# A spectral filter and a gated feed-forward network in one kernel: batch 1's first transform goes through DRAM, a quarter of it inside the feed-forward loop

## The chip, the cores and the metric

The kernel runs on one core of a Trainium2 chip. The metric is the device time of one execution in microseconds. TensorE (PE, with its weight loads PEld), VectorE (DVE), ScalarE (ACT) and GpSimd (POOL) each work through their own list of instructions in order; SyncE (SP) and POOL mostly issue DMAs here. They wait for each other through semaphores.

## The reference

```
X = rfft(x, axis=1)                    # x: 8 batches, 3008 positions, 256 columns d, float32
y = irfft(X * (filt_r + 1j*filt_i))    # a filter for each frequency and d
gate = maximum(y @ w_gate, 0)          # y as 24064 tokens x 256; w_gate, w_val: 256 x 1536
out  = (gate * (y @ w_val)) @ w_out    # w_out: 1536 x 256; out: 24064 x 256, float32
```

## The kernel before

**The transform.** The 3008 positions are taken as 94 (n1) by 32 (n2). For each batch: stage A is a 94-point transform over n1, for each n2; then its result must be turned, so that n2 lies on the partitions; `fwd` is the 32-point transform (six calls, i = 0 to 5, two PSUM banks each); `product` multiplies by the filter, `add` combines real and imaginary parts; `inv` (three calls, q = 0 to 2) goes back; its result is turned again, and `item_c` does the last 94-point step, which leaves the tokens as `yT` in blocks of 512, two halves of d each.

**The feed-forward network.** There are 47 blocks of 512 tokens with 12 steps each. A step is one `gv` (four matmuls of 512 columns into psV and psG, line 555; ACT copies psV as `vsb`, line 558; DVE makes `prod`, line 560) and, from the second block on, four matmuls of `o_part` for the block before (psO, line 576). Block k+1's `item_c` stands in steps 8 and 10 of block k (4 and 6 of block 0). Other work is hung on step numbers by `at_step(s, f)`; within a step the order is gv, o_part, the hung work, item_c. The schedule is written by hand: each engine takes its instructions in the order in which this program issues them.

**Three ways through stage A.** Batch 0 does it in the prologue with one float32 matmul for 512 columns (`a_bank`, line 265), ACT copies the result out (`a_0`, line 277) and DVE turns it (`turn_0`, line 300). Batches 2 to 7 do it inside the feed-forward loop in four chunks each. A chunk holds the columns n2 = 8q+2j and 8q+2j+1; `load_chunk` fetches it as two halves, the second in reversed row order (lines 340 and 344), into XP[j], a quarter of the buffers XF; POOL folds the halves in six instructions (`fold_chunk`, lines 353 to 358); `tiled_a` runs 32 small matmuls (psF, line 367), ACT and DVE copy two banks each, and SP stores the result to a buffer in DRAM (`Abuf`, line 378). When all four are there, `load_at_tiled` reads it back turned (line 385).

Batch 1 is between the two. Its x is loaded whole in the prologue, and 16 items `a_1`, of four n2 and half of d each, are spread by `item(n)` over batch 0's transform: two before inv(0,0), two before inv(0,1), two before inv(0,2), seven behind it, three behind the two `item_c` of block 0. The lower half of d goes through DRAM (`store_half`, line 324; `load_half`, line 330), the upper half is turned by DVE in four pieces (`turn_1`, line 295), one in the prologue and three in steps 1, 7 and 12. `fwd(1, 0)` and `fwd(1, 1)` stand in step 14.

**Batch 0 around the change.** `first_b` holds its six fwd and three inv. Products go to DVE from PSUM (line 422), those of `ON_POOL` to POOL (line 420), from a copy `xs` that ACT makes (line 419). `place_own` is two small copies on POOL (line 224); the third inverse block needs them. The results of inv(0, q) are copied to `DS0` (line 458), and `turn_d` turns all of it in two halves of d (line 300). POOL then issues the weight loads (`load_vg` twice, line 245, `load_o`, line 251), which convert to bf16 on the way, copies M1 (line 664) and changes the sign of every second row of Fti (line 672). `warm(n)` is n matmuls of 512 columns on a constant tile. `hold` is a small DMA on SP that waits for a part of the filter and so holds back batch 1's x.

Of the kernel before, what the change touches and what calls it, by code (L numbers as in the profile page):

```python
# [29 lines left out]
N1, N2 = 94, 32  # L30
# [86 lines left out]
def kernel(  # L117
# [44 lines left out]
    Abuf = [dram.tile([NROW * N2, D if b > 1 else D // 2], BF16, name=f"Abuf{b}") if b else None for b in range(B)]  # L162
# [9 lines left out]
    AS1 = [dCb[:, 32:48, :].rearrange("p n d -> p (n d)").rearrange("p (l c d) -> p l c d", l=NC2, d=D // 2)]  # L172
# [21 lines left out]
    WHOLE = ((0, 0, NX2 * D), (1, 0, NX2 * D))  # L194
# [3 lines left out]
    conj32 = pro.tile([128, 2], FP32, tag="conj32", bufs=1)  # L198
# [60 lines left out]

    def a_bank(n2, nn, d0, nd):  # L260

        psA = bank("psA", nn, nd)
        xf = XF[n2 // NX2].rearrange("p (n d) -> p n d", d=D)
        n = n2 % NX2
        nc.tensor.matmul(psA, WA, xf[:, n:n + nn, d0:d0 + nd], start=True, stop=True)  # L265
        return psA

    def a_0(n2, nn, d0, nd):

        psA = a_bank(n2, nn, d0, nd)  # L270
        dq = D // 4
        l, q = n2 % NC2, slice(d0 // dq, (d0 + nd) // dq)
        c = n2 // NC2
        dst = AS0.rearrange("p q (l c) e (g f) -> p l c g q e f", c=2, g=2)[:, l:l + nn, c // 2, c % 2]
        src = psA.rearrange("p n (q e f) -> p n q e f", e=dq // 2, f=2)
        for i in range(nd // dq):
            nc.scalar.copy(dst[:, :, q.start + i], src[:, :, i])
        done(psA)

    def a_1(p, s, h):  # L280

        psA = a_bank(NC2 * p + 4 * s, 4, h * D // 2, D // 2)
        if h and len(AS1) == 1:
            for _ in range(2):
                t = sb.tile([128, NC2 * D], BF16, tag="asb", bufs=3, name="asb")
                AS1.append(t.rearrange("p (l c d) -> p l c d", l=NC2, c=N2 // NC2))
        ts = AS1[1:] if h else AS1[:1]
        w = D // 2 // len(ts)
        for i, t in enumerate(ts):
            nc.scalar.copy(t[:, 4 * s:4 * s + 4, p, :], psA[:, :, i * w:(i + 1) * w])  # L290
        done(psA)

    def turn_a(dst, src):

        nc.vector.transpose(dst.bitcast(FP32).rearrange("p k d -> p d k"),
                            src.bitcast(FP32).rearrange("p n d -> p d n"))
# [6 lines left out]
    def turn_0(q):  # L303
        w = D // 8
        turn_pairs(ats[0][:, :, q * w:q * w + w], AS0[:, q])

    def turn_1(i):
        w = D // 8
        src = AS1[1 + i // 2].rearrange("p l c d -> p (l c) d")
        turn_a(ats[1][:, 1, :, i * w:i * w + w], src[:, :, i % 2 * w:i % 2 * w + w])  # L310

    def new_at(b):
        shape = [2, 32, D // 2] if b else [16, D // 2, 4]
        ats[b] = sb.tile([128, *shape], BF16, tag="at", bufs=1, name="at")
# [6 lines left out]
    def store_half(b):  # L321
        w = N2 * D // 2
        for q in range(4):
            nc.sync.dma_start(_ap(Abuf[b], q * NG * w, [[w, NG], [1, w]]),
                              AS1[0][32 * q:32 * q + NG].rearrange("p l c d -> p (l c d)"))

    def load_half(b):
        w = N2 * D // 2
        for q in range(4):
            nc.sync.dma_start(ats[b][32 * q:32 * q + 32, 0, 0:NG, :],  # L330
                              _ap(Abuf[b], q * NG * w, [[D // 2, 32], [w, NG], [1, D // 2]]))
# [3 lines left out]
    def load_chunk(b, j, eng):  # L335

        xp = XP[j]
        for q in range(4):
            r, o = 32 * q, 8 * q + 2 * j
            eng.dma_start(xp[r:r + 24, 0:4:2, :],  # L340
                              _ap(x, (b * N1 * N2 + o) * D,
                                  [[N2 * D, 24], [47 * N2 * D, 2], [1, 512]]))
        for i in range(2):
            eng.dma_start(xp[:, 2 * i + 1, :],
                              _ap(x, ((b * N1 + 46 + 47 * i) * N2 + 2 * j) * D,
                                  [[8 * D, 4], [-N2 * D, 32], [1, 512]]))

    def fold_chunk(b, j):

        xp = XP[j]  # L350
        t = fs.tile([128, 2, 512], FP32, tag="fold", bufs=1, name="fold")
# [29 lines left out]
    def load_at_tiled(b):  # L381

        ats[b] = sb.tile([128, NG, D], BF16, tag="at", bufs=1, name="at")
        for rr in range(4):
            nc.sync.dma_start(ats[b][32 * rr:32 * rr + 32].rearrange("p j d -> p (j d)"),
                              _ap(Abuf[b], rr * N2 * NG * D, [[NG * D, 32], [1, NG * D]]))

    ON_POOL = ((0, 1), (1, 1), (2, 1))
    ats = {}
# [3 lines left out]
    def fwd(b, i):  # L393
# [4 lines left out]
        for r in range(2):  # L398
            for c in range(4):
                for e in range(2):  # L400
# [3 lines left out]
                                     ats[b][64 * e:64 * e + 64, j, :] if b > 1 else  # L404
                                     ats[b][64 * e:64 * e + 64, :, j, :] if b else
# [3 lines left out]
    def product(b, i, e, k, pool=False):  # L409
# [6 lines left out]
        if pool:  # L416
            if not k:
# [17 lines left out]
    def inv(b, q):  # L435
# [14 lines left out]
        dst = sb.tile([128, 8, D], BF16, tag="dsb", bufs=3, name="dsb") if b else DS0  # L450
        def out(cs):
            for c in cs:
                copy = nc.vector.tensor_copy if (c % 2 if b else (q, c) in ((1, 3), (2, 0), (2, 1))) else nc.scalar.copy
                if b:
                    copy(dst[:, c:8:4, :], psD[c])
                else:
                    k, g = 4 * q + c // 2, c % 2 * 2
                    copy(dst[:, k:k + 3:2, :, g:g + 2], psD[c].rearrange("p m (f e) -> p m e f", f=2))
                done(psD[c])
        if not b:  # L460
            return out(range(4))
# [10 lines left out]
    def first_b(item):  # L472

        def products(i, es=(1, 0)):
            for e in es:
                for k in range(2):
                    product(0, i, e, k, pool=(i, e) in ON_POOL)
# [19 lines left out]
        place_own()  # L497
        inv(0, 1)
        item(2)
        inv(0, 2)  # L500

# [30 lines left out]
    def item_c(k, h):  # L532
# [10 lines left out]
        if h == 0 or k:  # L543
            nc.scalar.copy(dst, psY)  # L544
        else:
            nc.vector.tensor_copy(dst, psY)
# [88 lines left out]
    new_at(0)  # L635
# [11 lines left out]
    nc.sync.dma_start(hold, Ftr[0:2, 4, 0:8])  # L647
    load_x(1, sp, ((0, 0, 2 * q), (0, 2 * q, 4 * q), (1, 0, 2 * q), (1, 2 * q, 4 * q)))
    items = iter([(p, s, h) for p in range(4) for h in range(2) for s in range(2)])

    def item(n):
        for _ in range(n):
            p, s, h = next(items)
            a_1(p, s, h)
            if (p, s, h) == (3, 1, 0):
                new_at(1)
                store_half(1)
                load_half(1)

    first_b(item)  # L660
    load_vg(0, DFF // 2)
    load_vg(DFF // 2, DFF)
    load_o()
    nc.gpsimd.tensor_copy(M1, tabs[:, 578:].rearrange("p (l n) -> p l n", l=2))
    for h in range(2):
        turn_d(h)
    item(7)
    for hh in range(2):
        item_c(0, hh)
    item(3)  # L670
    turn_1(0)
    nc.gpsimd.tensor_scalar(Fti, Fti, conj[:, 0:1], 1.0, op0=ALU.mult, op1=ALU.mult)
    nc.sync.dma_start(WF, nc.inline_tensor(fold_h, name="dft_fold").ap())
# [9 lines left out]
    for k in range(1, 4):  # L683
        at_step((1, 7, 12)[k - 1], lambda k=k: turn_1(k))
# [77 lines left out]
```

## Time and profile before

| what | value |
|---|---|
| time, median of 3 runs | 867.87 us (867.31 to 867.9) |
| the profiled execution, its own time | 865.68 us |
| its span in the profile | 863.8 us |
| TensorE busy | 848.7 us, 98% of the span |
| DVE, ACT, POOL busy | 577.8, 494.6, 458.4 us |
| first psV matmul of the feed-forward network | 45.6 us |
| first psX matmul of batch 1 | 60.44 us |

The profile is of one execution. Times in it count from the start of the span. In the rows of the timeline and of the groups stand the start, the length in us, the engine, the line of the kernel, the operation, what it writes and reads, and in brackets the idle time of the engine before it and what ended it. SPq and POOLq are the parts of those engines that issue DMAs; a matmul in float32 shows as two records.

### The profile page before, as it was taken

To read this page: it belongs to the slowest core of one execution; us is meant where nothing else is said; L and a number is where in the kernel's file an instruction comes from. 1 tells how busy PE (TensorE), PEld (TensorE's weight loads), DVE (VectorE), ACT (ScalarE), POOL (GpSimd) and SP (SyncE) were. 2 spreads that over 40 slices of the span, in tenths; PEclk is the share of its full clock that TensorE was granted. 3 is DMA by queue.
4 is the path that set the end of the run, shared out by engine and by line. 5 is a ranking of instruction groups with operands and counts; after the bars stand their busy time and mean duration, and the time that the engine had idled before them with its cause. 6 is when DMAs were issued, how large, how long until landed. Compare 5 with 4: busy or idle time off the path is not lost.

```text
span 863.8 us, 20396 instructions
## 1 busy us (share of the span) xinstructions
PE 848.7 (98%) x7587; PEld 498.8 (58%) x7704; DVE 577.8 (67%) x863; ACT 494.6 (57%) x904; POOL 458.4 (53%) x496
## 2 busy tenths in 40 slices
PE   9999999999999999999999999999999999999997
PEld 4456655656556555556556655565655656666665
DVE  3878865777657775577765787658865688555553
ACT  5765565555655556555555555555556555555552
POOL 6747890488986765776666756767450023000001
PEclk9999999999999999999999999999999999999999
DMA  9985365334782339633386333762464422611111
GB/s 250 241 164 122 96 158 138 109 113 110 190 183 88 84 87 192 166 98 98 85 208 142 95 103 100 190 151 74 101 130 108 99 58 52 126 43 29 37 35 52
DMA packets 101366, 101.61 MB, mean 118 GB/s; under 512 B 21827, under 2 KB 89955, under 8 KB 99730
## 3 DMA queue, kind: packets, MB, share of 16 engines
q1 hardware_dynamic: 81986, 77.96, 36.1%
q0 software_dynamic: 18928, 21.82, 11.7%
q8 instruction: 61, 1.00, 0.5%
q10 hardware_dynamic: 352, 0.52, 0.2%
q14 instruction: 39, 0.32, 0.1%
HBM read 58.23 MB, written 45.88 MB: 121 GB/s over the span
## 4 chain that ended last, share of the span: by engine, by line
PE 94%; DMA 2%; issue 1%; DVE 1%; ACT 1%; SPq 1%; POOL 0%; DVEq 0%; ACTq 0%
PE psG L555 29%; PE psO L576 28%; PE psV L555 26%; PE psA L265 3%; PE psF L367 3%; PE psY L538 3%; PE psD L445 2%; PE psX L402 1%; DMA XF<-in_x_dram 1%; DMA Abuf<-asb 1%; ACT vsb L558 1%; DVE prod L560 1%; SPq L190 0%; DVE tt L422 0%; DMA out_dram<-osb 0%
## 5 line engine op out<-in xcount | busy, mean ns | idle before, releaser
L560 DVE SCALAR_TENSOR_TENSOR prod<-psG,vsb 128x512 bf16<-128x512 f32 x564 | 389.4, 691 | 235.8 <-ACT vsb L558 231.6
L558 ACT CAST vsb<-psV 128x512 bf16<-128x512 f32 x564 | 332.2, 589 | 225.8 <-PE psV L555 121.1
L576 PE MATMUL psO<-WoT,prod 128*128 128x256 bf16 x2256 | 336.6, 273 | 0.8
L555 PE MATMUL psG<-yT,WgT 128*128 128x512 bf16 x1111 | 331.8, 379 | 5.2
L555 PE MATMUL psV<-yT,WvT 128*128 128x512 bf16 x1030 | 314.9, 380 | 0.1
L576 PEld LDWEIGHTS <-prod 128*128 128x128 bf16 x2256 | 220.6, 98 | 143.4
L555 PEld LDWEIGHTS <-WgT 128*128 128x128 bf16 x1128 | 110.0, 97 | 133.5
L432 POOL TENSOR_TENSOR pp<-tt,uu 128x256 bf16<-128x256 f32 x84 | 60.9, 725 | 170.7 <-DVE uu L422 162.5
L555 PEld LDWEIGHTS <-WvT 128*128 128x128 bf16 x1128 | 100.3, 98 | 37.3 <-issue 25.6
L544 ACT CAST yT<-psY 128x512 bf16<-128x512 f32 x93 | 54.5, 586 | 43.2 <-PE psY L538 42.6
L589 ACT COPY osb<-psO 128x512 f32<-128x512 f32 x92 | 54.1, 588 | 22.1 <-PE psO L576 20.7
L600 POOL DMA_DIRECT2D out_dram<-osb x5 | 2.6, 534 | 119.6 <-ACT osb L589 118.0
L422 DVE TENSOR_TENSOR tt<-psX,Ftr 128x512 f32<-128x512 f32 (+1 forms) x93 | 63.5, 683 | 0.5 <-PE psX L402 0.5
L422 DVE TENSOR_TENSOR uu<-psX,Fti 128x512 f32<-128x512 f32 (+1 forms) x93 | 63.3, 681 | 0.3 <-DMA Fti<-in_filt_i_dram 0.3
L433 POOL TENSOR_TENSOR pp<-tt,uu 128x256 bf16<-128x256 f32 x84 | 60.9, 726 | 0.0
L353 POOL TENSOR_TENSOR fold<-XF 128x1024 f32<-128x1024 f32 x24 | 56.3, 2347 | 5.8 <-DMA XF<-in_x_dram 5.4
L354 POOL TENSOR_TENSOR XF<-XF 128x1024 f32<-128x1024 f32 x24 | 56.4, 2350 | 1.9
L257 POOL CAST scr<-prod 128x8 f32<-128x8 bf16 x19 | 3.6, 190 | 85.8 <-DVE prod L560 71.7
L340 POOL DMA_DIRECT2D XF<-in_x_dram x76 | 45.6, 602 | 2.0 <-issue 1.3
L374 ACT CAST asb<-psF 128x512 bf16<-128x512 f32 x48 | 25.8, 589 | 34.5 <-PE psF L367 34.5
L374 DVE CAST asb<-psF 128x512 bf16<-128x512 f32 x48 | 30.9, 686 | 18.0 <-PE psF L367 18.0
L538 PE MATMUL psY<-M,dCb 96*128 96x94 bf16 (+19 forms) x604 | 37.9, 200 | 0.0
(71 smaller groups left out, 457.8 us busy)
## 6 DMA issues: line engine op xcount, KB each, us to landing
Dbuf<-dsb SPq DMA_DIRECT2D x84, 128.0 KB
dCb<-Dbuf SPq DMA_DIRECT2D x56, 192.0 KB
XF<-in_x_dram POOLq DMA_DIRECT2D x38, 256.0 KB, 6.7
Abuf<-asb SPq DMA_DIRECT2D x96, 96.0 KB
at<-Abuf SPq DMA_DIRECT2D x24, 384.0 KB
XF<-in_x_dram SPq DMA_DIRECT2D x31, 256.0 KB
XF<-in_x_dram POOLq DMA_DIRECT2D x76, 96.0 KB, 5.1
out_dram<-osb SPq DMA_DIRECT2D x69, 94.0 KB
```

Of the source, the lines that this page charges most:

```text
L353: tt(t, xp[:, 0:2], xp[:, 2:4], op=ALU.add)
L354: tt(xp[:, 2:4], xp[:, 0:2], xp[:, 2:4], op=ALU.subtract)
L374: copy(asf[:, :, q, :], banks[q])
L422: nc.vector.tensor_tensor(p, psX, filt, op=ALU.mult)
L432: nc.gpsimd.tensor_tensor(p[:, 0], tt[:, 0], uu[:, 1], op=ALU.subtract)
L433: nc.gpsimd.tensor_tensor(p[:, 1], tt[:, 1], uu[:, 0], op=ALU.add)
L538: nc.tensor.matmul(psY[:, o:o + w], d_rows(b, n2, h), M1[:, 1, n1:n1 + w] if b == 0 else M1[:NROW, 0, n1:n1 + w], start=True, stop=True)
L544: nc.scalar.copy(dst, psY)
L555: nc.tensor.matmul(pt[:, :W], w[:, h, ft * 128:(ft + 1) * 128], yt[:, h, :], start=(h == 0), stop=(h == 1))
L558: nc.scalar.copy(vsb, psV[:, :W])
L560: nc.vector.scalar_tensor_tensor(prod, in0=psG[:, :W], scalar=0.0, in1=vsb, op0=ALU.max, op1=ALU.mult)
L576: nc.tensor.matmul(psO[:, t % 2], prods[ft][:, t * 128:(t + 1) * 128], WoT[:, ft, :], start=(ft == 0), stop=(ft == NFT - 1))
```

## The change

- Batch 1's stage A loses its columns n2 = 8p+6 and 8p+7. `load_x1` fetches only six of each eight columns, packed into 24 column places of XF, in 15 DMAs. `a_1(p, j)` takes two n2 and all of d: 12 items, two before inv(0,0), two before inv(0,1), one before inv(0,2), seven behind it, none behind the first item_c.
- The missing columns are chunk 3 of batch 1, done like the chunks of the later batches: its first half is issued by SP behind x (with the table WF), the mirrored half by POOL between the two halves of the weights, the fold comes on POOL behind the weight loads, `tiled_a(1, 3)` in step 6.
- All of batch 1's stage A goes through DRAM: `store_a1` in eight DMAs of 24 rows behind the last item, `load_at_tiled(1, 0, 24)` in step 1, `load_at_tiled(1, 24, 8)` in step 9. The four turns `turn_1` and the half-wise store and load go.
- The third inverse block of batch 0 is copied by halves of d: for each half four copies of half the size (for the first half two on ACT and two on DVE, for the second all on ACT), and `turn_d` of that half directly behind them. Of inv(0,1) ACT now makes all four copies.
- `ON_POOL` names the k as well: the second product of (4, 1) moves from DVE to POOL, behind a copy on ACT. POOL reaches `place_own` and the weight loads only after it.
- Smaller: the last copy and turn of batch 0's stage A are halved; each half of the first yT is copied by ACT and DVE together; `warm(2)` stands before and behind the first `item_c`; M1 is copied by ACT; Fti's sign change comes behind the fold; `hold` waits for the next part of the filter.

```diff
-    conj32 = pro.tile([128, 2], FP32, tag="conj32", bufs=1)
+    conj32 = consts.tile([128, 2], FP32)
...
+    def load_x1():
+        for p in range(4):
+            for o, w in ((0, 6),) if p != 2 else ((0, 4), (4, 2)):
+                t, s = divmod(6 * p + o, NX2)
+                for m in range(3):
+                    rows = min(32, N1 - 32 * m)
+                    nc.sync.dma_start(XF[t][m:m + 4 * rows - 3:4, s * D:(s + w) * D],
+                                      _ap(x, ((N1 + 32 * m) * N2 + NC2 * p + o) * D, [[N2 * D, rows], [1, w * D]]))
...
-            nc.scalar.copy(dst[:, :, q.start + i], src[:, :, i])
+            for e in (slice(0, 16), slice(16, 32)) if (n2, d0) == (24, 3 * dq) else (slice(0, 32),):
+                nc.scalar.copy(dst[:, :, q.start + i, e], src[:, :, i, e])
...
+    def a_1(p, j):
+        psA = a_bank(6 * p + 2 * j, 2, 0, D)
+        if j == 2 and len(AS1) == 1:
+            AS1.append(sb.tile([128, NC2 * D], BF16, tag="asb", bufs=3, name="asb").rearrange("p (n d) -> p n d", d=D))
+        i = 8 * (j % 2) + p
+        nc.scalar.copy(AS1[j // 2][:, i:i + 5:4, :], psA)
         done(psA)
...
+    def store_a1():
+        for t, o in zip(AS1, (0, 16)):
+            for rr in range(4):
+                nc.sync.dma_start(_ap(Abuf[1], (rr * N2 + o) * NG * D, [[D, NG], [NG * D, t.shape[1]], [1, D]]),
+                                  t[32 * rr:32 * rr + NG])
...
-    def load_at_tiled(b):
+    def load_at_tiled(b, o=0, n=N2):
+        if not o:
+            ats[b] = sb.tile([128, NG, D], BF16, tag="at", bufs=1, name="at")
         for rr in range(4):
-            nc.sync.dma_start(ats[b][32 * rr:32 * rr + 32].rearrange("p j d -> p (j d)"),
-                              _ap(Abuf[b], rr * N2 * NG * D, [[NG * D, 32], [1, NG * D]]))
+            nc.sync.dma_start(ats[b][32 * rr + o:32 * rr + o + n].rearrange("p j d -> p (j d)"),
+                              _ap(Abuf[b], (rr * N2 + o) * NG * D, [[NG * D, n], [1, NG * D]]))
-    ON_POOL = ((0, 1), (1, 1), (2, 1))
+    ON_POOL = {(0, 1): (0, 1), (1, 1): (0, 1), (2, 1): (0, 1), (4, 1): (1,)}
...
+        if not b:
+            w = D // 4
+            for h in range(2) if q == 2 else (0,):
+                for c in range(4):
+                    k, g = 4 * q + c // 2, c % 2 * 2
+                    e = slice(h * w, h * w + w) if q == 2 else slice(0, 2 * w)
+                    copy = nc.vector.tensor_copy if (q, h) == (2, 0) and c > 1 else nc.scalar.copy
+                    copy(DS0[:, k:k + 3:2, e, g:g + 2], psD[c].rearrange("p m (f e) -> p m e f", f=2)[:, :, e])
+                if q == 2:
+                    turn_d(h)
+            for c in range(4):
+                done(psD[c])
+            return
...
         place_own()
+        load_vg(0, DFF // 2)
         inv(0, 1)
-        item(2)
+        item(1)
         inv(0, 2)
+        nc.scalar.copy(M1, tabs[:, 578:].rearrange("p (l n) -> p l n", l=2))
...
-    nc.sync.dma_start(hold, Ftr[0:2, 4, 0:8])
-    load_x(1, sp, ((0, 0, 2 * q), (0, 2 * q, 4 * q), (1, 0, 2 * q), (1, 2 * q, 4 * q)))
+    nc.sync.dma_start(hold, Ftr[32:34, 4, 0:8])
+    load_x1()
+    load_chunk_fwd(1, 3, nc.sync)
+    nc.sync.dma_start(WF, nc.inline_tensor(fold_h, name="dft_fold").ap())
...
     first_b(item)
-    load_vg(0, DFF // 2)
+    load_chunk_back(1, 3, nc.gpsimd)
     load_vg(DFF // 2, DFF)
     load_o()
-    nc.gpsimd.tensor_copy(M1, tabs[:, 578:].rearrange("p (l n) -> p l n", l=2))
-    for h in range(2):
-        turn_d(h)
+    fold_chunk(1, 3)
+    nc.gpsimd.tensor_scalar(Fti, Fti, conj32[:, 0:1], 1.0, op0=ALU.mult, op1=ALU.mult)
     item(7)
+    store_a1()
+    warm(2)
     for hh in range(2):
         item_c(0, hh)
-    item(3)
-    turn_1(0)
-    nc.gpsimd.tensor_scalar(Fti, Fti, conj[:, 0:1], 1.0, op0=ALU.mult, op1=ALU.mult)
-    nc.sync.dma_start(WF, nc.inline_tensor(fold_h, name="dft_fold").ap())
+    warm(2)
...
-    for k in range(1, 4):
-        at_step((1, 7, 12)[k - 1], lambda k=k: turn_1(k))
+    at_step(1, lambda: load_at_tiled(1, 0, 24))
+    at_step(6, lambda: tiled_a(1, 3))
+    at_step(9, lambda: load_at_tiled(1, 24, 8))
```

## The prediction

> **What bounds the kernel now.** I read the page first: busy shares, then the chain that ended last.
>
> ```profile
> PE 848.7 (98%) x7587; PEld 498.8 (58%) x7704; DVE 577.8 (67%) x863; ACT 494.6 (57%) x904; POOL 458.4 (53%) x496
> ...
> PE 94%; DMA 2%; issue 1%; DVE 1%; ACT 1%; SPq 1%; POOL 0%; DVEq 0%; ACTq 0%
> ```
>
> TensorE is busy 98% of the span and carries 94% of the chain; its granted clock is full in all 40 slices. So an edit counts by the TensorE time it removes or adds, and by any wait it puts into TensorE's in-order queue. All of this change lies before 62 us. There I read the chain of waits from 26 to 47 us (start, length, what):
>
> ```profile
> 33.41 1.91 PE psA L265 x4
> 35.33 1.01 PE psD L445 x64
> 36.34 6.21 PE psA L265 x14
> 42.54 0.54 PE psY L538 x12
> 43.09 2.67 PE psA L265 x6
> 45.75 0.43 PE psV L555 x2
> ```
>
> This stretch is TensorE without a gap: stage-A items (psA), the inverse blocks (psD), the first output items (psY), and the FFN's first product at 45.6. Next the timeline of POOL, since a fold comes into it; the three last rows are a fold of batch 2, from its first instruction to what follows it:
>
> ```profile
> 29.30 1.15 POOL L420 TENSOR_TENSOR uu<-xs,Fti 128x512 bf16<-128x512 f32 x1
> 30.50 0.39 POOL L224 COPY I2t<-tabs 32x256 bf16<-32x256 bf16 x1
> 30.84 0.40 POOL L224 COPY I2u<-tabs 32x256 bf16<-32x256 bf16 x1
> 31.19 0.80 POOL L245 DMA_DIRECT2D WvT<-in_moe_w_val_dram  x1
> ...
> 34.12 1.69 POOL L251 DMA_DIRECT2D WoT<-in_moe_w_out_dram  x2
> 35.86 0.34 POOL L664 COPY M<-tabs 128x188 bf16<-128x188 bf16 x1
> ...
> 73.12 2.35 POOL L353 TENSOR_TENSOR fold<-XF 128x1024 f32<-128x1024 f32 x1
> ...
> 81.78 1.28 POOL L358 TENSOR_TENSOR XF<-fold 128x512 f32<-128x512 f32 x1
> 83.01 0.74 POOL L432 TENSOR_TENSOR pp<-tt,uu 128x256 bf16<-128x256 f32 x1
> ```
>
> A fold holds POOL from 73.12 to 83.01, 9.9 us. The view of the line that issues the mirrored half of an x chunk gives its landing, from issue:
>
> ```profile
> DMA to landing us min/median/max: 5.5/6.7/11.1
> ```
>
> Last, the DMA queue of SP, which carries batch 1's round trip through DRAM, and the busy time by stage of 40 to 46 us (its last columns: DMA share, GB/s):
>
> ```profile
> 44.68 2.79 SPq L324 DMA_DIRECT2D Abuf<-dCb  x4
> 47.68 3.59 SPq L330 DMA_DIRECT2D at<-Abuf  x4
> ```
> ```profile
> 40.00:46.00 6.00, 6.00 (x26) 2.61 (x25) 3.05 (x3) 4.39 (x11) 0.00 (x0) 1.00 1.33 201
> ```
>
> The stores go out at 44.68, the first load that needs one at 47.68, so a store lands 3.0 us after its issue; the last load is issued by 51.3, and fwd(1,0) uses the tile at 60.44: about 9 us of slack. Till 46 us the DMA engines are full at 201 GB/s.
>
> **TensorE, prologue.** Batch 1 has 12 items of 512 columns for 16. The three behind the output items are gone (2.66 us from 42.93 to 45.59), one of the two before inv(0,2) as well (0.9). Two warm(2) add 4 matmuls of 512 columns at 0.21 us: 0.9. Sum -2.7: the FFN starts at 42.9. The cover for the turned block holds: inv(0,2) ends near 35.4, the first copies by halves end at 36.1 (half of 0.6 each), two transposes of 2.36 run to 40.8, and the seven items keep TensorE till 41.5. Unsplit, the copies would end 1.4 after the inverse block, as now (36.3 to 37.7), and the transposes at 41.5: just in time. So the split brings 0.7 of slack and no time; if ACT were late with its second halves, each microsecond past 0.7 would be lost.
>
> **tiled_a(1,3).** 32 matmuls in a slot; in batch 2 such a slot goes from 120.53 to the next psV at 121.6: +1.1.
>
> **The fold's date.** This is where I expect the loss. The product uu(4,1) goes from DVE to POOL. It needs ACT to copy psX, and that copy stands behind the four copies of inv(0,0) (29.78, until 31.7), so it ends at 32.3 (0.6, row L419). POOL: product 1.15 to 33.4; place_own 0.7 to 34.2; first weight halves 1.5 to 35.7; the chunk's two mirrored loads 0.71 each to 37.1; second halves 1.4 to 38.5; WoT 1.7 to 40.3. Everything behind that product is 3 us later than now. The fold can't start before 40.3, nor before the chunk has landed: its second load is issued at 36.4, so at 41.9 by the shortest row, 43.1 by the median, 47.5 by the longest. It stands behind two weight loads, but no x transfer competes with these any more; I take 42.3, near the low end. Fold end: 42.3 + 9.9 = 52.2, bounds 50.2 (POOL alone) and 57.4. TensorE reaches tiled_a at 42.9 + 6.3 (45.59 to 51.88 now: seven gv and an output item) = 49.2, and all of the FFN is queued behind it. Wait: +3.0, bounds 1.0 and 8.2. Below nothing it can't be, unless POOL is a microsecond quicker than its rows.
>
> **The tile for fwd(1,0).** After tiled_a ends at 53.3: copies, two on each engine, 1.4 to 54.7; four stores, the third (which the first load needs) issued at 55.6 and landed 3.0 later, 58.6; four loads at 0.43 each, the last issued at 59.9. Its landing: between 1.9 us (an output at the very end, alone) and 5.0 (an x load behind two others, chain of waits at 21.69); I take 2.6: 62.5. TensorE has 8.56 us of work from tiled_a to fwd(1,0) (51.88 to 60.44): 61.9. Wait 0.6 if the queues are free. They aren't: from 41.3 on, the second weight halves and WoT (1.6 MB), the stores of 24 columns (1.2), their loads (1.2), tiled_a's store and load (0.4 each) make 4.8 MB, 24 us at 201 GB/s, to 65: a wait of 3. SP issues all of it in order, so the late store stands behind the loads of the first 24 rows. Bounds 0.6 and 3; I take 2.2, nearer the full queues, as these are full now at that point.
>
> A rule of the Trainium skill speaks against this part (DMA: Bandwidth & Descriptors, section Why a DMA increments its semaphore by 16 and not by 1): a transfer from SP is spread over the largest number of engines up to 16 that divides its row count, so 24 rows use 12 engines and the four loads of 8 rows all use the same 8. By it I estimate 1 to 2 us more in this wait, 872.5 to 873.5 in all; the trace of before has no load of 8 rows to show it.
>
> **Costed at nothing, with the cover.** The hold on Ftr[32:34] frees SP 0.5 us later (the two filter loads land 3.5 us after issue, issued 0.5 apart), but the first item now waits for 576 KB and not 768 (0.7 us at 281 GB/s); uncovered, 0.5. The halved last copy and turn of batch 0 end some 0.2 earlier, beside make_back_t, which holds TensorE until 22.2. DVE loses four transposes of 1.08 and takes two copies; TensorE was busy 8.95 of 9 us from 46 to 55, so nothing is to be had; if DVE were late there, 0.7. M1's copy on ACT (0.3) lies under the seven items. The sign change of Fti (2.8) comes after the fold, at 55, and is needed at 62. Batch 2's first chunk is issued some 2 us later; its fold at 73 had 9 us. The second weight halves, issued till 38.5, land near 46 (the third weight load now lands 7.9 after issue) and are needed at 48.3; should the stores slow them by more, that lies in the same wait as the fold's.
>
> **Sum.** -2.7 + 1.1 + 3.0 + 2.2 = +3.6. The profiled execution took 865.68 (its span of 863.8 and 1.9 around it), so its like after would be 869.3; it lies 2.19 under the median of 867.87, and on that I forecast 871.5.
>
> **Rivals.** *Both waits are hidden* (0.25): the fold ends by 49.2 and the tile is there at 59, so only -2.7 + 1.1 = -1.6 is left: 866.3, not slower. It decides on POOL: the fold must start by 39.3. For it: POOL was idle from 39 to 53. Against: the rows above add to 40.3 before any landing. *Only POOL counts* (0.12): the chunk has landed by 40.3, fold end 50.2, wait 1.0, second wait 0.6: ±0.0, 867.9. *The queues go deeper* (0.15): batch 2's chunk (0.9 MB) is issued from POOL in the same microseconds, and the mirrored load lands as late as its slower rows; second wait 4 to 5 and first 4: +6 to +8, 874 to 876. *The forecast* has 0.48, with 869.7 to 874 as its own range.
>
> **Numbers.** 0.2% is 1.7 us, about what a measurement of this kernel tells from no change: below 866.1 is faster, above 869.6 slower. The hidden case falls 0.15 below and 0.10 within, the POOL case within, the forecast 0.01 within and 0.47 above, the deep queues above: 0.15, 0.23, 0.62. A range from 866.3 to 875.2 leaves out about half of the hidden case and half of the deep one.
>
> **What would show it.** FFN's first psV at 42.9 (a later start would mean the turned block or the yT copies are late); POOL's weight issue at 34.2 and the fold's end at 52; TensorE idle before psF, put down to POOL, about 3 us; idle before the first psX of batch 1, put down to the load of its tile, about 2; nothing else moved up to the end. The prediction is wrong if the fold ends by 49, or if TensorE finds that tile landed.

## The result and the profile after

The changed kernel takes 898.87 us (median; 896.67 to 904.23), the kernel before on the same chip 867.88: a ratio of 1.0365 (95% interval 1.0319 to 1.0411). The forecast was 871.5 with a range up to 875.2: the direction was right, the size was not. The profiled execution took 898.77 us, with a span of 897.0.

The page after, busy row and chain (the same two lines as shown of before):

```profile
PE 856.0 (95%) x7615; PEld 500.5 (56%) x7732; DVE 574.0 (64%) x861; ACT 494.8 (55%) x903; POOL 470.8 (52%) x504
...
PE 86%; DMA 4%; issue 2%; POOL 1%; DVE 1%; ACT 1%; SPq 0%; ACTq 0%; DVEq 0%; POOLq 0%
```

TensorE is busy 7.3 us longer and idle 26 us longer; on the chain its share falls from 94 to 86%, while that of DMA rises from 2 to 4% and that of POOL from 0 to 1%. TensorE's waits from 20 to 110 us (who waited for whom: us in all, times, longest):

```profile
PE psX L405 <- DMA at<-Abuf: 18.2, 2, 15.8
PE psF L369 <- POOL XF L359: 4.0, 1, 4.0
PE psG L567 <- DMA WgT<-in_moe_w_gate_dram: 1.9, 1, 1.9
...
PE psV L567 <- DMA WvT<-in_moe_w_val_dram: 0.7, 1, 0.7
```

The two waits of the prediction are the two largest. The fold's has about the forecast size, the tile's is eight times its 2.2 us, and there are two for weights ahead of the fold's. (The fold's wait is for L359, the fifth of its six instructions.) The chain through that stretch (start, length, what) shows the two transfers that make the long wait:

```profile
50.89 2.35 POOL asb L355
...
59.60 3.32 PE psF L369 x32
...
65.52 18.01 DMA Abuf<-asb
...
84.76 6.08 DMA at<-Abuf
...
90.98 1.05 PE psX L405 x28
```

The tiled chunk's last store is issued at 65.52 and is awaited until 83.5; the prediction had 3.0 us for such a landing. The DMA queue of SP in the timeline shows that the eight earlier stores were slow as well:

```profile
43.87 7.37 SPq L320 DMA_DIRECT2D Abuf<-dCb  x4
51.34 6.15 SPq L320 DMA_DIRECT2D Abuf<-asb  x4
62.43 1.53 SPq L388 DMA_DIRECT2D at<-Abuf  x4
64.31 1.61 SPq L380 DMA_DIRECT2D Abuf<-asb  x4
82.81 2.22 SPq L388 DMA_DIRECT2D at<-Abuf  x4
```

Four stores took 2.79 us to issue before and take 7.37 now (one is held for 5.97 us), and the first load goes out at 62.43. That load needs the first and the fifth store. By the completions that the trace records, the first, issued at 43.87, is done at 54.95 and the fifth, issued at 51.34, at 62.35: 11 us each, where the prediction had 3.0. POOL's timeline, with its idle time and what ended it in brackets:

```profile
36.69 0.79 POOL L244 DMA_DIRECT2D WvT<-in_moe_w_val_dram  x1
37.48 0.73 POOL L244 DMA_DIRECT2D WgT<-in_moe_w_gate_dram  x1
38.20 1.46 POOL L342 DMA_DIRECT2D XF<-in_x_dram  x2
...
50.89 2.33 POOL L355 TENSOR_TENSOR asb<-XF 128x1024 f32<-128x1024 f32 x1 [8.13 <-DMA XF<-in_x_dram]
```

The mirrored loads are issued at 38.20 and the fold starts at 50.89; POOL sat idle for 8.13 us over it. Why all of these are late is seen in the busy time by stage (stage, length, then busy time of PE, PEld, DVE, ACT and POOL; the last three columns are the granted clock, the DMA engines' share, GB/s; the share adds up the times of all packets, so it can pass 1). First before, then after:

```profile
20.00:34.00 14.00, 12.37 (x339) 6.07 (x341) 13.21 (x21) 10.64 (x24) 10.30 (x13) 1.00 0.90 262
34.00:43.00 9.00, 9.00 (x95) 4.24 (x93) 6.42 (x5) 7.14 (x18) 4.96 (x5) 1.00 1.18 198
43.00:52.00 9.00, 8.95 (x45) 4.18 (x44) 6.20 (x9) 6.80 (x15) 0.00 (x0) 1.00 1.05 196
52.00:62.00 10.00, 9.89 (x87) 5.21 (x87) 8.48 (x13) 5.76 (x11) 7.16 (x13) 1.00 0.73 145
72.00:82.00 10.00, 9.89 (x119) 5.64 (x119) 7.29 (x12) 5.73 (x11) 9.77 (x8) 1.00 0.48 127
```
```profile
20.00:34.00 14.00, 11.77 (x273) 5.34 (x274) 11.77 (x20) 8.81 (x19) 7.14 (x7) 0.88 0.68 181
43.00:52.00 9.00, 8.08 (x48) 3.68 (x47) 5.01 (x9) 5.82 (x11) 1.11 (x1) 1.00 1.21 189
52.00:62.00 10.00, 4.04 (x36) 1.00 (x36) 1.03 (x2) 0.59 (x1) 9.76 (x7) 0.63 0.81 150
72.00:82.00 10.00, 0.36 (x4) 0.07 (x1) 0.69 (x1) 0.11 (x1) 2.67 (x5) 0.65 0.95 191
```

The change takes x transfers out of 20 to 34 us, where the DMA share falls from 0.90 to 0.68, and puts stores, loads and a chunk behind 43 us, where it was 1.05 until 52 us already. At 72 to 82 it is 0.95, for 0.48 before, while TensorE is idle for 9.6 of 10 us. The clock column shows a second cost: 0.63 and 0.65 where TensorE waits.

**Where the 32.7 us are.** Dates before and after at the same places of the program: step 6 (psF now, the first instruction behind it before) 51.88 and 59.60, so +7.7; psF's slot takes 3.1; fwd(1,0) at 60.44 and 88.13, of which 15.8 is the wait and 1.0 the low clock; batch 2's first psF at 112.9 and 145.6, another 5.0, 2.5 of it the second wait for the tile and the rest mostly low clock. Together 32.6; the forecast's terms for the same four places were 0.3, 1.1, 2.2 and 0.

### The profile page after: what moved, and what is told of

Same layout as the page of the kernel before. It is cut to its first block, busy times and chain, and to the rows that moved or that the text cites. A ratio compares the mean times of both kernels' runs of the same rounds, so it can differ in the third digit from the quotient of the medians.

```text
span 897.0 us, 20497 instructions
## 1 busy us (share of the span) xinstructions
PE 856.0 (95%) x7615; PEld 500.5 (56%) x7732; DVE 574.0 (64%) x861; ACT 494.8 (55%) x903; POOL 470.8 (52%) x504
## 4 chain that ended last, share of the span: by engine, by line
PE 86%; DMA 4%; issue 2%; POOL 1%; DVE 1%; ACT 1%; SPq 0%; ACTq 0%; DVEq 0%; POOLq 0%
PE psG L567 27%; PE psO L588 27%; PE psV L567 24%; PE psF L369 3%; PE psY L549 2%; DMA Abuf<-asb 2%; DMA at<-Abuf 2%; PE psD L447 1%; PE psX L405 1%; DVE prod L572 0%; ACT vsb L570 0%; DVE tt L424 0%; POOL XF L356 0%; POOL asb L355 0%; DMA out_dram<-XF 0%
## 5 line engine op out<-in xcount | busy, mean ns | idle before, releaser
L356 POOL TENSOR_TENSOR XF<-XF 128x1024 f32<-128x1024 f32 x25 | 58.8, 2353 | 2.0
L376 ACT CAST asb<-psF 128x512 bf16<-128x512 f32 x50 | 26.8, 589 | 44.2 <-PE psF L369 44.2
L335 POOL DMA_DIRECT2D XF<-in_x_dram x76 | 45.6, 602 | 4.2 <-DMA XF<-in_x_dram 2.7
L405 PE MATMUL psX<-at,F 64*32 64x256 bf16 x768 | 17.0, 280 | 21.6 <-DMA at<-Abuf 19.8
```

The costliest lines, as they stand in the source:

```text
L356: tt(xp[:, 2:4], xp[:, 0:2], xp[:, 2:4], op=ALU.subtract)
L376: copy(asf[:, :, q, :], banks[q])
```

## The experiments

Ratios are to the kernel before on the same chip (medians of 866 to 868 us). Dates are those of one profiled execution. Theory: *the DMA engines are full when the chunk and the round trip need them, and TensorE's order makes both due there.* Rivals: the halves of d; the place of one wait in POOL's or SP's order; the number of small pieces.

**1. No excursion.** All four quarters of x in the prologue, 16 items, all of stage A through DRAM in 12 stores, one load of 32 rows in step 1.

```diff
-    load_x1(); load_chunk_fwd(1, 3, nc.sync)
+    load_x(1, sp, ((0, 0, 2*q), (0, 2*q, 4*q), (1, 0, 2*q), (1, 2*q, 4*q)))
...
-    at_step(1, lambda: load_at_tiled(1, 0, 24)); at_step(6, tiled_a ...); at_step(9, ...)
+    at_step(1, lambda: load_at_tiled(1))
```

> The changed kernel without its excursion: x of batch 1 is loaded whole as before, 16 items in the prologue (7 before the first output items, 4 behind), all 32 columns stored in 12 DMAs of 24 rows and loaded back in one step; no fold and no chunk 3. Theory (the time goes into two TensorE waits that the excursion's chain of DMAs makes: the mirrored half queued behind weights, then store and load of the last 8 rows queued behind other transfers): the first wait is gone, the second is only one store and load of 1.6 MB, some 16 us from the last item, against 15 us of TensorE work: 870 to 880. Rival 'DRAM round trip of 512-byte rows': if the stores themselves are what is slow, most of the loss stays: 885 to 895.

877.75 us, 1.0114 (1.0095 to 1.0133). The round trip, with the small edits that this run keeps, costs 10 us, with 8.8 us of waits for the tile; the excursion the other 21. As expected.

**2. Only the halves of d**, put into the kernel before.

```diff
+        if not b:
+            for h in range(2) if q == 2 else (0,):
+                ...  # four copies of half the size, then turn_d(h)
...
-    for h in range(2):
-        turn_d(h)
```

> The kernel before with one part of the change only: the third inverse block of batch 0 copied and turned by halves of d; nothing of batch 1 is changed. If this part costs nothing, as the prediction had it, the time is that of before within 0.2% (866 to 869) and the first psV of the FFN stays at 45.6. If the four extra copies or the turns in other places hold the first output items, psY and the first psV come up to 1 us later (0.1% slower); if the earlier turn was worth anything, 0.1% faster. Either way it can't carry any large share of the 31 us.

867.38 us, 1.0001 (0.9987 to 1.0014); first psV at 45.67 for 45.59. This part costs and brings nothing, as the prediction had it.

**3. Batch 2's chunk loads later.**

```diff
-    loads, folds = ((6, 12, 20, 30), (22, 34, 46, 46)) if b == 2
+    loads, folds = ((15, 19, 24, 30), (26, 34, 46, 46)) if b == 2
```

> The changed kernel with batch 2's first two chunk loads moved from steps 6 and 12 to 15 and 19 (fold of the first from 22 to 26). Theory: the stores of tiled_a(1,3), 18 us from issue to landing, share the engines with these loads; without them they land within 6 us of the end of the 24-row loads, so TensorE's wait before the first psX of batch 1 falls from 18 to about 9 us: 888 to 892. Rival 'eight rows': if the 8-row loads and the place behind the 24-row loads make the wait, it stays above 14 us: 896 to 899.

892.84 us, 1.0292 (1.0256 to 1.0328). The chain of this run:

```profile
63.74 7.55 DMA Abuf<-asb
...
72.53 6.77 DMA at<-Abuf
```

The same store that was awaited for 18.01 us is awaited for 7.55, with nothing about it changed but what shares the engines with it. The waits for the tile fall from 18.2 to 7.9 us, and batch 2's first psF comes 10.3 us earlier (1.6 of them are an earlier first psV). In the total 6 of the 31 us were batch 2's x: some 4 are lost again behind that place, 2.1 of them in longer waits in batch 4. The time is just above the theory's 888 to 892.

**4. One load of 32 rows** in step 9, none in step 1, so that no load is in front of the tiled stores.

```diff
-    at_step(1, lambda: load_at_tiled(1, 0, 24))
...
-    at_step(9, lambda: load_at_tiled(1, 24, 8))
+    at_step(9, lambda: load_at_tiled(1))
```

> The changed kernel with batch 1's tile loaded in one piece of 4 DMAs of 32 rows in step 9, in place of 24 rows in step 1 and 8 rows in step 9. Theory 'eight rows' (each of the four 8-row loads runs on the same 8 engines, 1.5 us each, and the stores stand behind the 24-row loads): the stores land near 72 and not 83, the load of 1.6 MB then takes 8 to 10 us, fwd(1,0) starts near 82 and not 91: 888 to 891. Rival 'contention with batch 2's chunk': the stores land as late as now and the longer load adds 3: 900 to 903.

895.91 us, 1.0318 (1.0293 to 1.0343). The stores are awaited for 4.28 us now, but the load of four times the bytes, beside batch 2's chunk, for 14.51:

```profile
66.10 4.28 DMA Abuf<-asb
...
71.77 14.51 DMA at<-Abuf
```

Most of the gain went from the store into the load. The time lies between the two expected ranges, 5 us above the theory's.

**5. The mirrored loads ahead of the first weights.**

```diff
         place_own()
+        load_chunk_back(1, 3, nc.gpsimd)
         load_vg(0, DFF // 2)
```

> The changed kernel with the two mirrored loads of chunk 3 issued on POOL ahead of the first weight halves instead of behind them. Theory: the chunk lands 7 to 8 us after its issue, near 45 and not at 50.9, the fold starts when POOL has issued WoT (43) or at 45, and TensorE's wait before psF falls by 5 to 6 us; all behind it moves up by as much: 892 to 894. Rival 'POOL is the bound' (its product and issues, not the queue): the fold starts less than 2 us earlier: 897 to 899.

900.03 us, 1.0365 (1.032 to 1.041): a miss. The fold did start earlier, at 45.54, but TensorE paid elsewhere:

```profile
PE psX L405 <- DMA at<-Abuf: 23.0, 2, 20.4
PE psV L568 <- DMA WvT<-in_moe_w_val_dram: 3.0, 1, 3.0
PE psG L568 <- DMA WgT<-in_moe_w_gate_dram: 1.8, 1, 1.8
```

The weights are late by what the chunk is early, and the tile's wait grows, since its first load still goes out only at 61.4. So the fold's date does not set the end, and another place in POOL's queue beside the weights is no cure.

**6. The output weights behind the fold.**

```diff
-    load_o()
     fold_chunk(1, 3)
+    load_o()
```

> The changed kernel, with the two loads of the output weights (WoT, 1.6 MB in float32) issued by POOL behind the fold and not ahead of it. Theory: these loads share the DMA engines with the eight stores of batch 1's stage A from 43 to 62 us, and that is why the stores land at about 62 and not at 50. Without them the first load of the tile should come at 53 to 56, the stores of the tiled chunk are issued as now (64), and they find the 24-row loads already done: fwd(1,0) at 77 to 80 and 886 to 891 in all. Rival: what the stores need is set by their own 512-byte packets; then the first load comes at about 60 as now, and WoT, issued at 61 and later, competes with the tiled stores and holds o_part in step 12 as well: 897 to 905.

896.45 us, 1.0347 (1.0321 to 1.0373). The loads of the tile start at 55.00 instead of 62.43, as the theory had it (1.8 of the 7.4 us are an earlier first psV in this profile). But the tiled stores now meet the output weights: the last is awaited for 14.16 us, and o_part waits 2.1 us for them. The first loads came out as the theory had it; the time, 0.6 us under the rival's range, as the rival nearly had it.

**7. The same stores in big pieces**, each partition's 8 or 4 KB as one. This kernel leaves out the order in DRAM that the loads expect: it moves the same bytes, but batch 1's values are then not those of the reference.

```diff
-    _ap(Abuf[1], ..., [[D, NG], [NG * D, t.shape[1]], [1, D]])
+    _ap(Abuf[1], ..., [[n * D, NG], [1, n * D]])      # n = t.shape[1]
```

> The changed kernel, with the eight stores of batch 1's stage A writing the same bytes to the same part of the buffer, but each partition's 8 or 4 KB in one piece instead of 512-byte pieces; so batch 1's data in the buffer are in another order than the loads expect (its values are not the reference's). Theory: the number of 512-byte packets on engines shared with the weight loads is what makes the stores slow; then the stores land within 4 to 6 us of issue, the issue of the fourth is no longer held for 6 us, the mirrored loads and the weights land some us earlier as well (fold from 47, fwd(1,0) at 76 to 80), 884 to 890 in all. Rival: bytes and queue depth count, not pieces; then the first load of the tile still comes at about 61 and the time is 897 to 900.

897.39 us, 1.0334 (1.03 to 1.0367). The issue is no longer held (eight stores in 3.5 us), the first load goes out at 54.2, still 10 us behind the store that it needs last; and the output weights landed at 67.7 instead of 61.8. The profiled execution was the fastest of four (890.5 for up to 899.15), so its dates flatter it. Pieces of 512 bytes account for a held issue; the time they do not explain.

**8. Two small edits undone**: the hold on the earlier filter part, uu(4,1) on DVE.

```diff
-    nc.sync.dma_start(hold, Ftr[32:34, 4, 0:8])
+    nc.sync.dma_start(hold, Ftr[0:2, 4, 0:8])
-    ON_POOL = {..., (4, 1): (1,)}
+    ON_POOL = {...}
```

> The changed kernel, with two small edits undone: batch 1's x waits for the earlier part of the filter again, and the product uu(4,1) goes back to DVE. Theory: the lost 2.7 us of the prologue come from a pause of TensorE at the last filter part, after which the granted clock is 0.5 for about 3 us; that pause hangs on when the filters land beside x. If the place of the hold is what matters, the first item starts below 27 us at full clock and the first psV comes at 43 to 44. The product back on DVE brings the weight loads from 36.7 to about 33.5 and with them all of POOL's chain: fold 3 us earlier, the end at 894 to 896. Rival: the pause comes with x's smaller transfers or by chance of the queues; then the items start cold as now, psV stays at 45 to 46, and only the 3 us of POOL's chain are seen, or nothing, since SP's stores set the end.

900.12 us, 1.0373 (1.0341 to 1.0406). In the profiled execution (894.52, the fastest of four) the first psV comes at 43.28, the weights are issued at 31.46 and the fold starts at 46.82, and the stores are then as slow as ever: the last tiled store is awaited for 18.38 us. POOL 4 to 5 us earlier brings nothing: the first psV is the theory's, the time the rival's.

**9. Two loads of 16 rows** instead of 24 and 8.

```diff
-    load_at_tiled(1, 0, 24) ... load_at_tiled(1, 24, 8)
+    load_at_tiled(1, 0, 16) ... load_at_tiled(1, 16, 16)
```

> The changed kernel with the tile loaded as 16 and 16 rows and not as 24 and 8; the second load still waits for the tiled stores. Under the rule that 8 rows use 8 engines and 16 rows 16, the four second loads take as long as before with twice the bytes: 1.5 us from one landing to the next, the last some 6 us after the first is issued, fwd(1,0) and the total within 1 us of the changed kernel's. If bytes set the time, they take 3 us each, and the total is 5 to 6 us longer.

One execution, 900.2 us, within 1.4 of the changed kernel; but the second loads ran beside batch 2's chunk (awaited for 14.73 us), so this is no clean measure of engines against rows. It shows something else: with the smaller load in front, the last tiled store is awaited for 8.38 us and not 18.01, although batch 2's chunk is beside it as before.

**10. The whole chunk on SP**, taken out of POOL's order among the weights, with the later chunk loads of run 3 and the single load of run 4.

```diff
-    load_chunk_fwd(1, 3, nc.sync)
+    load_chunk(1, 3, nc.sync)
```

> The changed kernel with three edits: the mirrored half of the chunk is issued by SP with the other half, ahead of all weights; batch 2's chunk loads in steps 15, 19, 24, 30; one load of the tile with all 32 rows in step 9, none in step 1. Theory: the two waits of the changed kernel are both made by transfers that stand or share engines with others, so both shrink. The chunk lands by 41, the fold runs from about 40 (POOL, behind the weights) to 50, psF has no wait over 1 us; the tiled stores are issued at 53 to 58, right behind the other stores, and all land by 60 to 62; the four loads of 32 rows take 6 us; fwd(1,0) at 67 to 70 for 60 without a wait: 876 to 882 in all. Rival: the queue needs the same time for the same bytes in whatever order they are issued; then fwd(1,0) stays at 76 or later and the time above 888.

887.44 us, 1.0234 (1.0191 to 1.0277). Issued at 35.30 to 36.6, the mirrored half is awaited until 53.3, 17 us: later than behind the weights on POOL. It was not ahead of all weights, since POOL issued its first at 34.41. The trace records the completion of each of these two loads in 4 parts only (47.1 to 48.2 and 52.4 to 53.2 us), for 12 of a load of 24 rows. So its shape, four blocks of rows in reverse, may be a reason; no run varies it. The waits trade places, 10.9 for the fold and 5.0 for the tile:

```profile
PE psF L369 <- POOL XF L359: 10.9, 1, 10.9
PE psX L405 <- DMA at<-Abuf: 5.0, 2, 3.4
```

Its gain over the changed kernel, 11 us, is about that of runs 3 and 4 together (6 and 3), and little is left for an issue 2.9 us earlier.

**11. As 10, and fwd(1,0) five steps later** (the other groups 3 and 1).

```diff
-    starts, gap = ((-37, -25, -13), 4) if b == 1
+    starts, gap = ((-32, -22, -12), 4) if b == 1
```

> As the kernel with the chunk on SP and one load of the tile, and besides batch 1's three groups of fwd, products and inv start 5, 3 and 1 steps later (fwd(1,0) in step 19 and not 14), and batch 2's chunk loads in steps 19, 22, 26, 30. Theory: the round trip through DRAM is not wrong in itself, only due too early; 5 steps are worth 7 us, so the wait at fwd(1,0) is 0 to 3 us, and the time is 867 to 873; with both waits gone it would show the 1.6 us that the work taken out of the prologue is worth (866). Rival: batch 1's later end is late for block 5 (its results go through DRAM as well, and now have five steps for it), and a wait there of several us takes the place of the one removed: 875 or more.

885.31 us, 1.0173 (1.011 to 1.0236); the four executions lie between 875.45 and 886.42. No wait for the tile is left, and 10.56 us for the fold: the expectation missed because the chunk was as late as in run 10.

**12. The whole trip later**, the mirrored loads on POOL: tiled_a in step 11, the load in 13, fwd(1,0) in 19, and the two edits of run 8 undone.

```diff
+    at_step(11, lambda: tiled_a(1, 3))
+    at_step(13, lambda: load_at_tiled(1))
...
+    starts, gap = ((-32, -22, -12), 4) if b == 1
+    loads, folds = ((19, 22, 26, 30), (30, 36, 46, 46)) if b == 2
```

> The changed kernel with the whole trip of batch 1 moved later, the mirrored loads on POOL as they were: tiled_a in step 11 (was 6), one load of 32 rows in step 13 (for 24 in step 1 and 8 in step 9), fwd(1,0) in step 19 (14; the other two groups 3 and 1 later), batch 2's chunk loads in steps 19, 22, 26, 30, and the two small edits undone (the hold on the earlier filter part, the product uu(4,1) on DVE). Theory: the chain fold, store, load is as long as in the changed kernel, some 22 us from the fold's start at 47 to the tile at 69 to 72, but TensorE now asks for the fold's result at about 55 and for the tile at 66 to 68; what is left is 1 to 2 us for weights that land late, 0 to 1 for the fold and 2 to 4 for the tile, against 1.6 us less work: 869 to 873. Rival: the chain moves along with its own due dates (SP issues the tiled stores only behind tiled_a), or the clock falls in each wait: 876 or more. If the wait at fwd(1,0) is nil, 866 to 868, which would be as fast as before.

883.14 us, 1.0187 (1.0154 to 1.0221). The theory's 869 to 873 is missed by 10 us. The waits are small (fold none, tile 3.5, weights 1.2), yet batch 2's first psF comes 14.2 late. The items of block 3 were 8.4 late at 94.7 us and those of block 4 14.2 late at 117.9. In between POOL folds batch 2's chunk while inv of batch 1 waits for its adds; the next run asks whether that is the cause.

**13. As 12, with batch 2's folds between batch 1's groups.**

```diff
-    loads, folds = ((19, 22, 26, 30), (30, 36, 46, 46)) if b == 2
+    loads, folds = ((17, 25, 29, 33), (27, 37, 47, 47)) if b == 2
```

> The run with the whole trip later, and batch 2's folds moved to steps 27, 37, 47, 47 (were 30, 36, 46, 46), between batch 1's groups of adds, its chunk loads to steps 17, 25, 29, 33. Theory: the 5.8 us lost between the second and third block (89 to 121 us) came from a fold of 9.9 us that held POOL when inv of batch 1 waited for its adds; with it between the groups that loss goes: 876 to 878. Rival: the chunk's transfers, not POOL, slow that stretch; then it stays at 881 to 884.

878.74 us, 1.0123 (1.0095 to 1.0151), 4.4 us less. From block 3's items to block 4's 0.9 us are lost now for 5.8, and TensorE's waits for POOL's adds (psD on pp) fall from 2.9 to 1.0 us. That speaks for POOL, though batch 2's chunk loads moved too, by two or three steps. The total is a little above the expected 876 to 878.

**14. As 13, and the mirrored loads early**, at 28.5 us, in the slack; tiled_a in step 7, the load in step 12.

```diff
         for i in range(3):
             fwd(0, i)
             if i < 2:
                 products(i)
+        load_chunk_back(1, 3, nc.gpsimd)
```

> As the run before this one, and the chunk's two mirrored loads issued on POOL behind products(1), at about 29 us, ahead of all weight loads; tiled_a in step 7, the load of the tile in step 12. From 20 to 34 us the DMA engines are 0.7 busy, from 34 to 62 full. Theory: in the slack the mirrored loads land by 38 to 40, the fold runs from 38 to 47, ahead of TensorE, the tiled stores go out with the others and the tile is there at 66, ahead of step 19: no wait at psF, none over 1 us at psX, some 1 us for weights; 866 to 870 in all, about the time of before. Rival: the bytes are the same and the engines are full till 62 anyway; then the weights or the stores come later by as much, TensorE waits 3 to 6 us for weights or for the tile, and the time is 873 or more.

874.4 us, 1.0077 (1.0054 to 1.01), the fastest version with an excursion and still 0.8% behind the kernel before. POOL's timeline, and the stage 20 to 34:

```profile
28.54 1.42 POOL L342 DMA_DIRECT2D XF<-in_x_dram  x2
...
43.15 2.35 POOL L355 TENSOR_TENSOR asb<-XF 128x1024 f32<-128x1024 f32 x1 [5.51 <-DMA XF<-in_x_dram]
```
```profile
20.00:34.00 14.00, 12.07 (x272) 5.51 (x274) 11.81 (x19) 8.77 (x19) 10.27 (x13) 0.88 0.78 197
```

The mirrored loads land in 6.0 and 7.6 us here, for 11.8 in the changed kernel, and neither psF nor the weights keep TensorE waiting; the tile does for 1.0 us. So the waits are the theory's, but the time is the rival's (873 or more). (The fold still starts at 43.15 and not at 38: now SP's half of the chunk, issued at 33, lands last.) Batch 2's first psF is 4.8 us late, and the span is 10 longer: what is left is small waits and, at 377 us, one of 2.9 in batch 4, which comes up at that place (1.1 to 3.4 us) in most runs with the excursion and whose cause is open.

**15. Mirrored loads early, dates of the changed kernel** (tiled_a in step 6, one load in step 9, fwd(1,0) in step 14, batch 2's loads as in run 3, the two edits of run 8 undone).

```diff
-    at_step(1, lambda: load_at_tiled(1, 0, 24)); ...; at_step(9, lambda: load_at_tiled(1, 24, 8))
+    at_step(9, lambda: load_at_tiled(1))
+        load_chunk_back(1, 3, nc.gpsimd)        # in first_b, behind products(1)
```

> The mirrored loads early as in the run before this one, the two small edits undone, one load of 32 rows in step 9, batch 2's chunk loads in steps 15, 19, 24, 30, but tiled_a in step 6 and fwd(1,0) in step 14 as in the changed kernel. Theory: the fold's wait is nil, and the tile comes at about 66 for a TensorE that asks at 58 to 59: a wait of 6 to 8 us and 1 to 2 of low clock behind it, 875 to 878. Rival (the stores land only when all weights are in, whatever the fold does): tile at 70 or later, 880 or more.

880.17 us, 1.0147 (1.0122 to 1.0172); the rival's number, by a hair. No wait at psF over 0.4, and 6.6 for the tile. So the place of the mirrored loads, one load, a free queue and the undone edits together take back 19 of the 31 us, and the later dates of run 14 6 more.

## Why the prediction was wrong

**The tile (forecast +2.2, measured 16.8 and 5.0).** This is the step that failed. It took the landing of a store from one row of before, 3.0 us from issue; here the first and the fifth store took 11 us each, so that the load behind them went out 18.6 us after the first was issued, and the last tiled store took 18. The step did see that the queues are full and set 4.8 MB against 201 GB/s, to end at 65. Three things were wrong with that. The row of before did not carry over, although the engines' share was above 1 there too. What differed is which queue held them (packets, MB, share of the 16 engines' time; q0 is POOL's, q1 SP's): before from 44.7 to 47.7 us, after from 43.9 to 55, after from 72 to 82.

```profile
q1 hardware_dynamic: 60, 0.39, 58.6%
q0 software_dynamic: 373, 0.18, 45.4%
```
```profile
q0 software_dynamic: 1617, 1.60, 96.8%
q1 hardware_dynamic: 760, 0.38, 16.6%
```
```profile
q0 software_dynamic: 1082, 1.55, 77.1%
q1 hardware_dynamic: 746, 0.36, 17.9%
```

Before, POOL's loads were through at 46.9, when the first store was on its way; now they last until 61.8, and batch 2's chunk follows. Then, the step counted batch 2's chunk only in a rival, although that is issued in the same microseconds; run 3, which moves it, shortens the late store from 18.0 to 7.6 us and the kernel by 6. The chunk alone does not do it: without the 24-row loads in front (run 4) the store takes 4.3, with smaller ones (run 9) 8.4, chunk and all. And the step took the end of the transfers as the end of the wait. The trip is a chain of three: first stores, tiled stores, loads. SP issues them in this order, and the first loads, like the last, start only when the stores that they need have landed. Runs 4 and 6 show that shortening one link while the queues are full lengthens another. The rival that named it, *the queues go deeper*, gave it 4 to 5 us; right in its mechanism, a quarter of the size.

Behind it stands a unit. The profile counts a weight load at the size it writes (384 KB for each of the six), and from 28 to 46 us these converting loads and the mirrored ones moved 1.31 MB in 48.4% of the engines' time, SP's transfers 1.63 MB in 33.3%: 1.8 times the time for a byte. So GB/s over a mixed stage is no rate to which further bytes may be added. The engines' share says more, and it stood at 1.18 and 1.05 from 34 to 52 us already before.

**The fold's date (forecast 52.2, measured 59.6).** POOL reached the second mirrored load at 38.9 and not at 36.4, since it had waited 4.18 us for ACT's copy before its product uu(4,1), which began at 34.77, for a forecast of 32.3. The landing was taken near its shortest row, 5.5 us, with the reason that no x transfer competes. It took 11.8, with the weights in the same queue. (psF needs five of the fold's six instructions, 8.7 us for the forecast 9.9; that gave 1.2 back.) Runs 5, 10 and 14 show the landing elsewhere: ahead of the weights at 34.7 it still needed 10 us and the weights paid; on SP 17; at 28.5, on engines with slack, 6.0 and 7.6. That the wait in the table, 4.0, is near the forecast 3.0 is luck: TensorE was 6 us late itself.

**The prologue (-2.7, measured +0.1).** The edits do bring the FFN forward: in nine of the fourteen profiles with the shorter prologue (run 5's counted without its wait for weights) the first psV comes at 43.3 to 44.2, for 45.6 before and a forecast of 42.9. In the profile of the changed kernel it comes at 45.67. There the last filter part landed at about 24.2 (23.5 before), TensorE paused for 1.78 us (0.98 before), and the items that followed ran at half clock:

```profile
28.00:31.00 3.00, 3.00 (x4) 0.82 (x3) 3.00 (x6) 0.59 (x1) 2.60 (x3) 0.55 0.52 158
```

The clock column is 0.55, for 1.00 in the same stage before. Four of the profiles behind the change show it (the changed kernel and runs 4, 14 and 15), with a first psV at 45.5 to 46.2; run 1, with the longer prologue, shows it too. (The fourteenth, run 13, has 44.7 at full clock.) What separates them is not settled: run 2's pause at that place was 1.24 us with a clock of 1.00, run 14's 0.79 with 0.56.

**tiled_a's slot (1.1, measured 3.1).** Its 32 matmuls come behind 4.0 us of waiting and run at the low clock; in run 14, without the wait, the chain has them at 1.07.

**The Trainium skill's rule** (DMA: Bandwidth & Descriptors, section Why a DMA increments its semaphore by 16 and not by 1) spreads a transfer from SP over the largest number of engines up to 16 that divides its row count: 12 for 24 rows, 8 for 8. The trace agrees: behind the issue it records 12 completions for each load of 24 rows and 8 for each load of 8 rows. The prediction had estimated 1 to 2 us from it. The four loads of 8 rows are done at 86.60, 88.09, 89.67 and 90.84, one after another by 1.2 to 1.6 us although the engines are only 0.32 busy in that stage (82 to 92 us). It is a small part of the loss. The Trainium skill, on the same page in the section Queues, rings and completion order, says that each DMA engine takes its queues in turn, packet by packet. That fits a store which grows from 7.6 to 18 us with what else is queued, and no run here shows the engines' order itself.

**What held.** The halves of d at nothing (run 2); the sign; the two places of the waits and the engines they were put down to; that nothing further would move, but for 1.6 us in batch 4 and for the two waits for weights, 2.6 us together, which came ahead of the fold's and not within it.

## What to carry to other kernels

Before moving a transfer, read not only the DMA engines' share in the stage where it will run, but also which queue holds them and for how long. Here the share was above 1 both where a store landed in 3.0 us and where one took 11; POOL's queue had 45% of the engines' time in the one place and 97% in the other. While such a queue lasts, reordering mostly chooses who waits. A chain of dependent transfers can pay for it again at each link, so count the links as well as the bytes, and give the chain its slack in steps of the engine that needs it. Look for the slack by stage: here it lay at 20 to 34 us, and one pair of loads moved into it, with the chain's steps drawn forward behind it, took 4.3 us off the best reordering (run 14 against run 13).

## What the hardware showed

A mirrored load of the same 256 KB, from issue to landing, took 6.0 and 7.6 us where the DMA share was 0.83 (run 14, 28.5 to 37 us), 11.8 where it was 0.9 to 1.2, and about 17 when SP issued it. SP's issue itself can be held: the like of a store that needs 0.3 us to issue held the queue for 5.97 us, and with it everything SP had to issue after it. That was with pieces of 512 bytes; with pieces of 8 and 4 KB all eight stores were issued in 3.5 us (run 7). And a wait costs TensorE more than its length: behind the 18 us the granted clock was 0.5 until about 95 us, and the stretch to batch 2's first psF lost 2.5 us beyond the waits.
